# Eleven conversion turns from the last batch to earlier ones, and another order of work in the last batch

## The chip, the cores and the metric

The kernel runs on one core of a Trainium2 chip. The metric is the device time of one execution in microseconds (us), as the median of several runs. Five engines work side by side: TensorE (PE in the profile, PEld for its weight loads), VectorE (DVE), ScalarE (ACT), GpSimd (POOL) and SyncE (SP), which here issues transfers (DMA).

## The reference

Inputs are q, k, v of 8 batches x 8 heads x 576 rows x 64, and weights. Three layers follow one another, in float32:

```python
q_s = softmax(q, over the head's 64);  k_s = softmax(k, over the 576 rows)
x = q_s @ (k_s.T @ v)                      # each head, heads side by side: 576 x 512
h = gelu(x @ w_in)                         # tanh form; w_in is 512 x 1024
u, v = h[..., :512], h[..., 512:]
v_n = (v - mean(v)) / sqrt(var(v) + 1e-6) * g_ln
x = x + (u * (w_sg @ v_n + b_sg)) @ w_out  # w_sg is 576 x 576
xt = x.transpose(0, 2, 1)                  # second block
u = x + (xt @ U @ V).transpose(0, 2, 1)    # U, V of rank 32
out = u + relu(u @ w_ch1) @ w_ch2          # w_ch1 is 512 x 2048
```

The weights arrive as 64-bit floats, so each has to be converted on the chip.

## The kernel before, in words

**Numbers.** Every product is made of three matmuls: an operand is split into a high part (a ScalarE copy to fp32r) and a low part (`low`, a subtraction on VectorE or GpSimd), and high x high, high x low and low x high are added in PSUM (`prod`, line 577).

**Phase one** runs once for each of the 8 batches (`for b in range(B)`, line 1321), each batch in the same stages: the V half of the first product with gelu and statistics (`emit_Vh`, `stats`, `emit_ln`), in 5 tiles of rows; in the same loop, called the passage here, the transposes of the batch before (`emit_yT`), its product with U (`emit_U`, which leaves the tile pst) and with V (`emit_PV`, which leaves PSUM tiles pw, adds them to yt and stores it in `u2d`); then the U half (`emit_Uh`, PSUM tile pu, gelu on ScalarE), the spatial product (`emit_S`, PSUM tile pS; its gate is a multiplication on VectorE, or on GpSimd for the columns in `GATES_POOL`; `split_G` makes the parts gh and gl), and the output product (`emit_y`, PSUM tile py; a VectorE addition makes yt). For the next batch, softmax work, the transposes of q (pt, ql) and the first product (`emit_xT`, px) lie between.

PSUM tiles come from `ps2`, three buffers of two banks (pv, pw, pu, pS, py, pt, px, pm), and `ps1`, two of one bank. A tile's first matmul waits until its buffer's last reader is done.

**Phase two** makes the channel product with seven products instead of eight for each 2 x 2 block: `steps` is a list of 280 steps of 12 matmuls, over five groups of columns, i = 0 for w_ch1 and i = 1 for w_ch2. The letters a = 1 to 7 name the products. A step waits for its weights (`wu`, five buffers, fetched five steps ahead from `wd`). The first seven steps (PSUM tile pm) run in the last batch's part of the loop, mixed with that batch's own transposes and U and V products (`pvs`). Their operands for group 0 (`uh`, `ul`) are made by the generator `u_first` (line 842), called as `prep`, in 26 pieces which the last batch's code takes with `next(prep, None)`. `H_SUMS`, `h_prep` and `u_side` do the same kind of work for later steps.

**Conversions.** w_ch1 and w_ch2 are converted in 16 rounds of 11 items (`conv_ch`): four blocks (load, clamp on GpSimd, exponent on ScalarE, merge in two VectorE instructions, lines 183 and 184) and seven factors (for some a sum on GpSimd or VectorE, then a high part on ScalarE, a low part on GpSimd or VectorE as `DVE_FACTOR_LOWS` says, and a store into `wd`). A turn (`T`) moves the pipeline by one item: it issues one operation of each kind, for items up to six apart (`LATE`). `TURNS[b]` says how many turns stand in each slot of batch b: five slots in the V loop, four each in the U, S and y stages, and up to five in the first product of the next batch; row 0 counts other pieces. `STEP_TURNS` and `GROUP_TURNS` do so for phase two.

**What sets the order.** TensorE runs in written order throughout, VectorE throughout the batches (`in_order(dve)`), all of them in the later steps of phase two. ScalarE, GpSimd and SyncE are otherwise put in order by a planner with its own estimates. Each engine and SyncE's queue run their instructions in order, so one that waits holds those behind it. In this document batches count from 1 to 8; `b` counts from 0.

## Time and profile before

| | before |
|---|---|
| median of 3 runs | 1292.64 us (1290.99 to 1294.96) |
| the profiled execution | 1292.16 us |
| its span, first to last instruction | 1290.4 us |
| TensorE busy | 1261.8 us, 98% |
| VectorE busy | 969.8 us, 75% |
| ScalarE busy | 653.3 us, 51% |
| GpSimd busy | 324.3 us, 25% |
| granted TensorE clock, mean | 0.989 |

The profile is of one execution; times within it count from its first instruction. A busy time says how much of the span an engine worked, not whether anything waited for it; for that the views by stretch and in order of time are needed. By those, batch 8 runs from about 519 us to 586 us, where the first step of phase two starts, and the eighth step starts at 613 us. Ends of matmuls are modelled, so that they overlap their successors, and "idle before" counts from such an end.

### The profile page before, as it was taken

To read this page: it belongs to the slowest core of one execution; us is meant where nothing else is said; L and a number is where in the kernel's file an instruction comes from. 1 tells how busy PE (TensorE), PEld (TensorE's weight loads), DVE (VectorE), ACT (ScalarE), POOL (GpSimd) and SP (SyncE) were. 2 spreads that over 40 slices of the span, in tenths; PEclk is the share of its full clock that TensorE was granted. 3 is DMA by queue.
4 is the path that set the end of the run, shared out by engine and by line. 5 is a ranking of instruction groups with operands and counts; after the bars stand their busy time and mean duration, and the time that the engine had idled before them with its cause. 6 is when DMAs were issued, how large, how long until landed. Compare 5 with 4: busy or idle time off the path is not lost.

```text
span 1290.4 us, 20684 instructions
## 1 busy us (share of the span) xinstructions
PE 1261.8 (98%) x7628; PEld 1142.8 (89%) x7628; DVE 969.8 (75%) x1406; ACT 653.3 (51%) x998; POOL 324.3 (25%) x421
## 2 busy tenths in 40 slices
PE   6999999999999999999999999999999999999998
PEld 5798999999998989797887888888888889999998
DVE  6898889797988888788769943597347953694485
ACT  5756667675757576754563512443224522451342
POOL 4734152623333334663630202000200002000000
PEclk8899999999999999999999999999999999999999
DMA  8515161715343352568998676678766788898786
GB/s 271 167 55 167 51 207 51 235 51 167 99 158 117 113 170 76 195 202 284 397 346 295 213 257 235 220 246 281 259 189 224 256 286 303 274 314 302 256 297 212
DMA packets 135909, 274.17 MB, mean 212 GB/s; under 512 B 15232, under 2 KB 56704, under 8 KB 135808
## 3 DMA queue, kind: packets, MB, share of 16 engines
q1 hardware_dynamic: 135808, 272.84, 64.0%
q8 instruction: 61, 1.00, 0.3%
q14 instruction: 40, 0.33, 0.1%
HBM read 224.56 MB, written 48.23 MB: 211 GB/s over the span
## 4 chain that ended last, share of the span: by engine, by line
PE 82%; DVE 8%; DMA 4%; ACT 3%; issue 1%; POOL 1%; SPq 1%; DVEq 0%; POOLq 0%; ACTq 0%
PE mm L52 51%; PE pS L52 8%; PE py L52 6%; PE pv L52 5%; PE pu L52 5%; PE px L52 1%; PE pk L52 1%; PE pt L553 1%; PE pt L741 1%; PE pp L52 1%; DVE bst L644 1%; DVE sh L654 1%; DMA wu<-wd 1%; DVE yt L55 1%; PE pm L52 1%
## 5 line engine op out<-in xcount | busy, mean ns | idle before, releaser
L52 PE MATMUL mm<-oh,wu 128*128 128x512 f32 (+1 forms) x1120 | 320.5, 367 | 1.2 <-DMA wu<-wd 1.2
L52 PE MATMUL mm<-uh,wu 128*128 128x512 f32 (+1 forms) x1064 | 303.4, 366 | 0.0
L52 PEld LDWEIGHTS mm<-oh,wu 128*128 128x128 f32 x1120 | 207.1, 188 | 27.6 <-ACT oh L61 1.6
L52 PEld LDWEIGHTS mm<-uh,wu 128*128 128x128 f32 x1064 | 196.6, 188 | 24.1 <-issue 0.2
L52 PE MATMUL mm<-ol,wu 128*128 128x512 f32 (+1 forms) x560 | 205.5, 367 | 0.0
L61 ACT ACTIVATE oh<-h 128x1024 fp32r<-128x1024 f32 (+1 forms) x140 | 135.2, 973 | 125.3 <-PE mm L52 104.6
L52 PE MATMUL mm<-ul,wu 128*128 128x512 f32 (+1 forms) x532 | 194.7, 366 | 0.0
L55 DVE TENSOR_TENSOR ol<-h,oh 128x1024 fp32r<-128x1024 f32 (+1 forms) x140 | 156.4, 1121 | 40.1 <-ACT oh L61 37.2
L55 POOL TENSOR_TENSOR ust<-ust 128x1024 f32<-128x1024 f32 (+1 forms) x16 | 36.3, 2278 | 384.5 <-DMA ust<-u2d 323.6
L55 DVE TENSOR_TENSOR h<-mm,u 128x1024 f32<-128x1024 f32 (+1 forms) x57 | 63.3, 1111 | 83.8 <-PE mm L52 83.8
L52 PEld LDWEIGHTS mm<-ol,wu 128*128 128x128 f32 x560 | 105.1, 188 | 13.2
L55 DVE TENSOR_TENSOR u<-mm,u 128x1024 f32<-128x1024 f32 (+1 forms) x53 | 58.9, 1111 | 73.2 <-PE mm L52 68.1
L52 PEld LDWEIGHTS mm<-ul,wu 128*128 128x128 f32 x532 | 99.9, 188 | 12.1
L55 POOL TENSOR_TENSOR chw<-f,chw 128x256 fp32r<-128x256 f32 x98 | 80.7, 836 | 97.6 <-ACT chw L61 87.6
L55 DVE TENSOR_TENSOR h<-h,h 128x1024 f32<-128x1024 f32 (+1 forms) x80 | 88.9, 1111 | 0.1
L1102 ACT ACTIVATE h<-mm 128x1024 f32<-128x1024 f32 (+1 forms) x19 | 17.8, 938 | 128.3 <-PE mm L52 128.3
L1093 ACT ACTIVATE h<-h 128x1024 f32<-128x1024 f32 (+1 forms) x60 | 58.1, 969 | 33.6 <-DVE h L55 33.6
L61 ACT ACTIVATE chw<-f 128x256 fp32r<-128x256 f32 x112 | 42.5, 411 | 63.6 <-DVE f L184 30.7
L61 ACT ACTIVATE u<-mm 128x1024 f32<-128x1024 f32 (+1 forms) x24 | 22.5, 936 | 96.3 <-PE mm L52 80.0
L171 POOL TENSOR_SCALAR stg<-stg 128x256 f32<-128x256 f32 (+1 forms) x88 | 44.3, 508 | 91.3 <-DMA stg<-in_w_ch_dram 50.4
L52 PE MATMUL pu<-xh,wih 128*128 128x288 f32 x256 | 57.9, 308 | 1.9 <-ACT wih L61 0.6
L52 PE MATMUL pu<-xh,wil 128*128 128x288 f32 x256 | 56.3, 301 | 1.8 <-DVE wil L55 1.8
(177 smaller groups left out, 2661.8 us busy)
## 6 DMA issues: line engine op xcount, KB each, us to landing
wu<-wd SPq DMA_DIRECT2D x280, 512.0 KB, 4.4
wd<-chw SPq DMA_DIRECT2D x112, 256.0 KB, 3.5
stg<-in_w_ch_dram SPq DMA_DIRECT2D x64, 256.0 KB, 3.5
u2d<-yt SPq DMA_DIRECT2D x32, 288.0 KB, 2.3
vt<-in_v_dram SPq DMA_DIRECT2D x32, 256.0 KB, 6.9
qt<-in_q_dram SPq DMA_DIRECT2D x7, 1024.0 KB, 8.2
kt<-in_k_dram SPq DMA_DIRECT2D x7, 1024.0 KB, 6.4
res<-u2d SPq DMA_DIRECT2D x12, 512.0 KB, 5.8
```

The source lines that it names most:

```text
L52: pe.matmul(out, lhsT, rhs, start=first, stop=last, skip_group_check=onto)
L55: return eng.tensor_tensor(out=out, in0=a, in1=b, op=op)
L61: return act.activation(out, src, AF.Copy)
L171: eng.tensor_scalar(out=hi, in0=hi, scalar1=F64_MOST, scalar2=-F64_MOST, op0=ALU.min, op1=ALU.max)
L553: pe.transpose(pt[:, t * P : (t + 1) * P], qt[:, t, c * P : (c + 1) * P], ident)
L644: dve.bn_stats(out=bst[0:n], in_=ge[0:n])
L654: dve.scalar_tensor_tensor(out=shift[0:n], in0=mv[0:n, 0:1], scalar=-1.0, in1=mv[0:n, 1:2], op0=ALU.mult, op1=ALU.mult)
L741: pe.transpose(pt[0:n, c * P : (c + 1) * P], y_t[b][:, c, t * P : t * P + n], ident)
L1093: act.activation(h, h, AF.Relu)
L1102: act.activation(h_out(j, 11, n), bank, AF.Relu)
```

## The change

- `TURNS`: batches 2 to 5 get two turns more each and batch 6 three, all in the y stage; the last batch has 18 turns instead of 29, none in its S stage.
- The first slot of the y stage comes behind the first `emit_y` in all batches but the last.
- The last batch gets a branch of its own for the V loop: `emit_U` and `emit_PV` are called right behind `emit_Vh`, ahead of `stats`; the layer norm of tile 2 comes ahead of the slot.
- In the last batch ScalarE is put in written order from the U stage to the y stage (`acts`).
- `GATES_POOL` of the last batch is empty: all four gates on VectorE.
- `emit_y` of the last batch makes columns 0 and 1 together: three of the four parts of both, then the last part of both.
- `u_first` takes tile vh4 instead of vl3 for its fourth operand, and the parts for a = 5 of its second half come behind the low part for a = 4. Its pieces are taken at other places: 1 instead of 3 ahead of the second U product, 5 ahead of the first S product instead of 2 behind it, 1 instead of 2 behind the S stage, and the rest behind step 2's `pvs` instead of within step 2.
- The norm of the last rows (`ln_scale`, `ln_split` of tile 4) comes one U product later.
- Of steps 4 to 6 the turns come behind `pvs`.

```diff
-    GATES_POOL = ((), (2,), (2,), (2,), (2,), (2,), (2,), (2,))
+    GATES_POOL = ((), (2,), (2,), (2,), (2,), (2,), (2,), ())
...
+        cols = (c,) if b < B - 1 or c > 1 else (0, 1)
+        if c == cols[0]:
+            for x in cols:
+                py_t[x] = ps2.tile([P, 2, 512], F32, tag="big", name="py")
+            for fcs in (range(NF - 1), range(NF - 1, NF)):
+                for x in cols:
+                    cs = slice(x * P, (x + 1) * P)
+                    for fc in fcs:
+                        prod(py_t[x], wo_h[:, fc, cs], wo_l[:, fc, cs], gh[:, fc], gl2[:, fc], fc == 0, fc == NF - 1)
+        py = py_t.pop(c)
         tt(dve, two(y_t[b][:, c]), halves(py), two(x_t[b][3][:, c]), ALU.add)
...
-            parts = [wrk.tile([P, F], F32, tag=x, name="us") for x in ("vh2", "vl2", "vh3", "vl3")]
+            parts = [wrk.tile([P, F], F32, tag=x, name="us") for x in ("vh2", "vl2", "vh3", "vh4")]
...
                 tt(dve, u22, u22, u11, ALU.subtract)
-                high(5, u22)
-                yield
-                rest(5, u22)
                 yield
                 rest(4, u21)
+                yield
+                high(5, u22)
+                rest(5, u22)
                 yield
...
-        (('T', '', '', '', ''), ('', '', '', ''), ('T', 'T', 'TTT', 'TT'), ('TT', 'TTTT', 'TTW', ''), ('', '', '', '', '')),
-        (('', '', '', '', ''), ('', '', '', ''), ('', 'TT', 'TT', 'TT'), ('TTT', 'TTTT', 'TT', 'T'), ('', '', '', '', '')),
-        (('', '', '', '', 'T'), ('T', '', '', ''), ('', 'TT', 'TTT', 'TTT'), ('TT', 'TTT', 'T', ''), ('', '', '', '', '')),
-        (('', '', '', '', ''), ('P', '', '', ''), ('', 'TT', 'TT', 'TT'), ('TTT', 'TT', 'TT', 'T'), ('', 'T', '', '', '')),
-        (('', '', '', '', ''), ('', 'B', 'T', 'T'), ('', 'TB', 'TTT', 'TT'), ('T', 'TT', 'TT', 'T'), ('', '', '', '', '')),
+        (('T', '', '', '', ''), ('', '', '', ''), ('T', 'T', 'TTT', 'TT'), ('TT', 'TTTT', 'TTTW', 'T'), ('', '', '', '', '')),
+        (('', '', '', '', ''), ('', '', '', ''), ('', 'TT', 'TT', 'TT'), ('TTT', 'TTTT', 'TTT', 'TT'), ('', '', '', '', '')),
+        (('', '', '', '', 'T'), ('T', '', '', ''), ('', 'TT', 'TTT', 'TTT'), ('TT', 'TTT', 'TT', 'T'), ('', '', '', '', '')),
+        (('', '', '', '', ''), ('P', '', '', ''), ('', 'TT', 'TT', 'TT'), ('TTT', 'TTT', 'TTT', 'T'), ('', 'T', '', '', '')),
+        (('', '', '', '', ''), ('', 'B', 'T', 'T'), ('', 'TB', 'TTT', 'TT'), ('TT', 'TTT', 'TT', 'TT'), ('', '', '', '', '')),
...
-        (('TTT', 'TT', 'TT', 'T', 'TT'), ('TT', 'T', 'T', 'TTT'), ('TT', 'T', 'TT', ''), ('TTT', 'TT', 'PT', 'T')),
+        (('TTT', 'TT', 'TT', '', 'TTT'), ('T', 'T', '', ''), ('', '', '', ''), ('TT', 'TT', 'PT', 'T')),
...
+        else:
+            for t in range(NT + 1):
+                emit_Vh(b, t)
+                if t == 2:
+                    for t2 in range(NT + 1):
+                        emit_U(b - 1, t2)
+                for c in ((), (), (), (0, 1), (2, 3))[t]:
+                    emit_PV(b - 1, c)
                 stats(b, t)
+                if t >= NT - 1:
+                    emit_ln(b, t - 1)
+                slot(TURNS[b][0][t])
+                if 0 < t < NT - 1:
+                    emit_ln(b, t - 1)
                 for t2 in ((2,), (3, 4), (), (), ())[t]:
                     emit_yT(b - 1, t2)
...
+            acts = in_order(act)
+            acts.__enter__()
...
-                for _ in range((0, 3, 3, 3)[f]):
+                for _ in range((0, 1, 3, 3)[f]):
                     next(prep, None)
...
-            if not nxt and f == 1:
+            if not nxt and f == 2:
                 ln_split(b, NT)
...
-            if not nxt and f == 0:
+            if not nxt and f == 1:
                 ln_scale(b, NT)
...
+            if not nxt:
+                for _ in range((5, 0, 0, 0)[f]):
+                    next(prep, None)
             emit_S(b, f)
...
-            if b or c:
+            if c or not nxt:
                 with tc.issue_after(last['s'].ins) if not nxt and c == 0 else contextlib.nullcontext():
                     slot(TURNS[b][3][c])
             emit_y(b, c)
-            if b == 0 and c == 0:
+            if nxt and c == 0:
                 slot(TURNS[b][3][c])
...
+            acts.__exit__(None, None, None)
             close_wo()
...
-                for _ in range((1, 0, 9, 0, 0, 0, 0)[s]):
+                for _ in range((1, 0, 0, 0, 0, 0, 0)[s]):
                     next(prep, None)
-                slot(STEP_TURNS[s])
+                if s < 4:
+                    slot(STEP_TURNS[s])
...
                 pvs(s)
-                for _ in range(2 if s == 1 else 0):
+                for _ in range((0, 2, 9, 0, 0, 0, 0)[s]):
                     next(prep, None)
+                if s >= 4:
+                    slot(STEP_TURNS[s])
```

## Rows read from the trace of the kernel before

**Rows 1.** The page, part 1: busy us (share of the span) and instructions of each engine.

```profile
PE 1261.8 (98%) x7628; PEld 1142.8 (89%) x7628; DVE 969.8 (75%) x1406; ACT 653.3 (51%) x998; POOL 324.3 (25%) x421
```

**Rows 2.** Busy us by stretch (PE, PEld, DVE, ACT, POOL), clock, DMA share, GB/s.

```profile
450.60:519.30 68.70, 68.48 (x531) 64.54 (x530) 59.52 (x113) 46.80 (x79) 26.54 (x37) 1.00 0.41 137
...
519.30:560.00 40.70, 38.50 (x237) 34.26 (x236) 31.25 (x59) 30.78 (x61) 27.38 (x37) 1.00 0.52 178
```

**Rows 3.** TensorE in order of time: start, duration, instruction [idle before, what ended it].

```profile
539.05 0.80 PE L52 MATMUL pw<-v_w,pst 128*128 128x288 f32 x4 [0.26 <-DVE pst L55]
...
543.27 0.53 PE L52 MATMUL pw<-v_w,pst 128*128 128x288 f32 x2 [1.29 <-DVE yt L55]
...
546.70 0.43 PE L52 MATMUL pu<-xl,wih 128*128 128x288 f32 x2
546.96 0.43 PE L52 MATMUL pu<-xh,wil 128*128 128x288 f32 x2
547.85 0.53 PE L52 MATMUL pu<-xh,wih 128*128 128x288 f32 x2 [0.46 <-DVE yt L55]
...
574.99 0.53 PE L52 MATMUL py<-gl,wo_h 128*128 128x288 f32 x2 [0.51 <-DVE gl L55]
...
586.06 0.63 PE L52 MATMUL pm<-uh,wu 128*128 128x512 f32 x2
...
596.94 0.73 PE L52 MATMUL pm<-uh,wu 128*128 128x512 f32 x2 [0.76 <-ACT h L1102]
...
609.24 0.77 PE L52 MATMUL pw<-v_w,pst 128*128 128x288 f32 x2 [0.40 <-DVE yt L55]
```

**Rows 4.** VectorE in order of time, the passage of the last batch.

```profile
537.02 1.25 DVE L654 SCALAR_TENSOR_TENSOR sh<-mv 128x1 f32<-128x1 f32 x1
...
540.96 1.39 DVE L184 SCALAR_TENSOR_TENSOR f<-stg,f 128x256 uint32<-128x256 uint32 x1
...
542.46 1.42 DVE L55 TENSOR_TENSOR yt<-pw,yt 128x576 f32<-128x576 f32 x2
...
547.06 1.40 DVE L55 TENSOR_TENSOR yt<-pw,yt 128x576 f32<-128x576 f32 x2
```

**Rows 5.** GpSimd in order of time, the last batch.

```profile
540.69 1.38 POOL L55 TENSOR_TENSOR vl<-ge,vh 128x512 fp32r<-128x512 f32 x1
...
569.92 1.86 POOL L55 TENSOR_TENSOR gt<-gt,ut 128x576 f32<-128x576 f32 x1 [0.35 <-DVE gt L708]
```

**Rows 6.** VectorE in order of time, the y products of the last batch.

```profile
574.18 1.59 DVE L55 TENSOR_TENSOR gl<-gt,gh 128x576 fp32r<-128x576 f32 x2
...
584.25 0.75 DVE L55 TENSOR_TENSOR yt<-py,x 128x576 f32<-128x576 f32 x1
```

**Rows 7.** ScalarE in order of time, step 2 of phase two.

```profile
595.35 0.63 ACT L61 ACTIVATE uh<-us 128x512 fp32r<-128x512 f32 x1 [1.10 <-DVE us L55]
595.88 1.01 ACT L1102 ACTIVATE h<-pm 128x1024 f32<-128x1024 f32 x1
```

**Rows 8.** The chain that ended last: start, us, what; steps 4 and 5.

```profile
608.15 1.04 DVE yt L55 x2
```

**Rows 9.** Who waited for whom, TensorE: us in total, times, longest.

```profile
PE mm L52 <- DMA wu<-wd: 1.2, 1, 1.2
```

**Rows 10.** Groups of VectorE instructions, batches 2 to 7: count, busy, mean ns, idle before.

```profile
L184 DVE SCALAR_TENSOR_TENSOR f<-stg,f 128x256 uint32<-128x256 uint32 x36 | 18.7, 521 | 1.2
...
L183 DVE TENSOR_SCALAR f<-f 128x256 uint32<-128x256 uint32 x36 | 15.7, 435 | 0.1
...
L55 DVE TENSOR_TENSOR chw<-f,chw 128x256 fp32r<-128x256 f32 x14 | 11.2, 799 | 1.8 <-POOL f L55 1.7
```

**Rows 11.** VectorE in order of time, the y stage of batch 4.

```profile
310.06 0.94 DVE L55 TENSOR_TENSOR chw<-f,chw 128x256 fp32r<-128x256 f32 x1 [1.73 <-POOL f L55]
...
313.80 0.76 DVE L55 TENSOR_TENSOR yt<-py,x 128x576 f32<-128x576 f32 x1 [0.67 <-PE py L52]
```

**Rows 12.** TensorE in order of time, the same stage.

```profile
315.20 0.60 PE L741 MATMUL pt<-ident,yt 128*128 128x128 f32 x4
```

More of the change, by code (lines that the diff above doesn't have):

```diff
@@ L720, in fused_kernel @@
     y_t = {}
+    py_t = {}
     def emit_y(b, c):
@@ L725, in emit_y @@
         gh, gl2 = g_t[b]
-        py = ps2.tile([P, 2, 512], F32, tag="big", name="py")
-        cs = slice(c * P, (c + 1) * P)
-        for fc in range(NF):
-            prod(py, wo_h[:, fc, cs], wo_l[:, fc, cs], gh[:, fc], gl2[:, fc], fc == 0, fc == NF - 1)
+        cols = (c,) if b < B - 1 or c > 1 else (0, 1)
[8 more added lines that the diff above has]
+        py = py_t.pop(c)
         tt(dve, two(y_t[b][:, c]), halves(py), two(x_t[b][3][:, c]), ALU.add)
@@ L1337, in fused_kernel @@
             load_ahead()
-        for t in range(NT + 1):
-            emit_Vh(b, t)
-            if nxt:
-                with behind(dve):
-                    for t2 in Q_MAX[b > 0][t]:
-                        q_max(nxt, t2)
-                    for _ in range(FOLDS[b > 0][t]):
-                        next(fold)
-            if t < NT:
-                stats(b, t)
-            slot(TURNS[b][0][t])
-            if t > 0:
-                emit_ln(b, t - 1)
-            if t == NT:
-                stats(b, t)
-            if b > 0:
+        if nxt:
+            for t in range(NT + 1):
+                emit_Vh(b, t)
+                if nxt:
+                    with behind(dve):
+                        for t2 in Q_MAX[b > 0][t]:
+                            q_max(nxt, t2)
+                        for _ in range(FOLDS[b > 0][t]):
+                            next(fold)
+                if t < NT:
+                    stats(b, t)
+                slot(TURNS[b][0][t])
+                if t > 0:
+                    emit_ln(b, t - 1)
+                if t == NT:
+                    stats(b, t)
+                if b > 0:
+                    for t2 in ((2,), (3, 4), (), (), ())[t]:
+                        emit_yT(b - 1, t2)
+                if t == 2 and b > 0:
+                    for t2 in range(NT + 1):
+                        emit_U(b - 1, t2)
+                if b > 0:
+                    for c in ((), (), (), (0, 1), (2, 3))[t]:
+                        emit_PV(b - 1, c)
+        else:
+            for t in range(NT + 1):
+                emit_Vh(b, t)
+                if t == 2:
+                    for t2 in range(NT + 1):
+                        emit_U(b - 1, t2)
+                for c in ((), (), (), (0, 1), (2, 3))[t]:
+                    emit_PV(b - 1, c)
+                stats(b, t)
+                if t >= NT - 1:
+                    emit_ln(b, t - 1)
+                slot(TURNS[b][0][t])
+                if 0 < t < NT - 1:
+                    emit_ln(b, t - 1)
                 for t2 in ((2,), (3, 4), (), (), ())[t]:
                     emit_yT(b - 1, t2)
-            if t == 2 and b > 0:
-                for t2 in range(NT + 1):
-                    emit_U(b - 1, t2)
-            if b > 0:
-                for c in ((), (), (), (0, 1), (2, 3))[t]:
-                    emit_PV(b - 1, c)
         spread_at = 2 if b else 3
@@ L1447, in fused_kernel @@
                     k_exp(nxt, ((0, 1, 2), (3, 4))[f])
-            if not nxt:
-                for _ in range((2, 0, 0, 0)[f]):
-                    next(prep, None)
             if f > 0:
@@ L1457, in fused_kernel @@
             with tc.issue_after(last['s'].ins):
-                for _ in range(2):
+                for _ in range(1):
                     next(prep, None)
```

## Prediction

> **What bounds the kernel now.** I began with the busy times of the page: TensorE is busy for 98% of the span, the others for 75% or less [rows 1]. A busy TensorE only bounds the whole if it is busy everywhere, so I went on to busy times by stretch. In a middle batch it works 68.48 of 68.70 us: nothing can be won there, and anything that makes it wait is paid in full. In the head of the last batch it works 38.50 of 40.70 us [rows 2]. So the matmul count sets the time, and what a reordering can win is the sum of TensorE's waits from the last batch to the first steps of phase two.
>
> The third view is TensorE's instructions in order of time there, with the idle time ahead of each. Six waits stand out: 0.26 (pw, for VectorE's pst), 1.29 (pw, for VectorE's yt), 0.46 (pu, for yt), 0.51 (py, for gl), 0.76 (pm, for ScalarE's h) and 0.40 us (pw, for yt) [rows 3], 3.68 us in all. Two corrections: ends are modelled, so idle time starts late (pairs at 546.70 and 546.96 start 0.26 us apart though each lasts 0.43, so 0.17 is to be added to each wait), and the first pair after a wait takes 0.53 instead of 0.43 us [rows 3], 0.10 more. With 0.27 for each of six the purse is 3.68 + 1.62 = 5.3 us: 2.82 in the passage (0.26 + 1.29 + 0.46 + 0.81), 0.78 at the y products, 1.03 and 0.67 in the steps. It is 0.41% of the time. Four of the six end with VectorE, so its queue, which is in order, is the second view: what stands in it ahead of the instruction that TensorE waits for.
>
> **Passage reordered, additions first.** The last batch's V loop gets its own branch. TensorE's order stays; what changes is VectorE's. Before, the low part of pst stood behind the shift sh, which took 1.25 us from 537.02 to 538.27; and the first two additions yt stood behind statistics and a conversion merge that took 1.39 us from 540.96; they ran from 542.46 to 543.88. The other two ran at 547.06, behind the statistics of the last tile [rows 4]. Afterwards pst comes ahead of statistics and conversions, the pair of additions right behind V tile 3's products, the next pair right behind tile 4's. The slot of the fourth turn is empty, so no merge stands there. pst then needs no cover: it waits for its own ScalarE copy alone, and I expect its 0.43 us gone. The additions can start when their own pw is there (the first pw runs at 539.05 [rows 3]), if VectorE is free. It has statistics 2, two merges and one sh still to do, which it did before pst in the old order and now does behind it. The pair would so end near 541.5 instead of 543.88, just when pw and pu ask for the PSUM buffers (the pw that waited restarted at 543.27 after 1.29 us idle [rows 3], so it asked near 541.8). The third wait (pu at 547.85) goes too: its addition moves ahead of statistics. What is late next is the statistics and layer-norm of tiles 2 and 3; they are wanted by the S products, which follow four pu groups later, and these cover them. I take 2.3 of 2.82 us, because the two additions come just in time rather than early; bounds 0.8 (one merge and one sh stretched as in [rows 4]: about 0.9 and 1.1 us) and 3.1 (the pu restart after the second pw included).
>
> **Gate 2 of the last batch on VectorE, y products in pairs.** The gate took 1.86 us on GpSimd [rows 5]; a VectorE instruction of that size takes 0.75 us (yt at 584.25 [rows 6]). Because of the late gate two low parts gl came in a bunch, 1.59 us from 574.18 [rows 6], and py waited 0.51 us idle for the first. Now gl of column 2 comes a S group earlier, and py of columns 0 and 1 run three of their four parts (36 matmuls) before they ask for the last gl. Each effect covers the wait alone: 0.75 of 0.78 us, bounds 0.4 and 0.78. The price is that the first y addition is ready later, as its product ends with the pair. Its cover: the second addition, which frees the buffer that pm takes, ended at 585.00 while pm started at 586.06 [rows 3, 6], 1.06 us to spare; one turn and one low part (ul) fewer stand ahead of it now, so I cost it at nothing; without the cover it would cost up to 1 us.
>
> **Preparation of group 0's first operands.** `u_first` keeps its work; five instruction groups come ahead of S product 0 instead of around it, and the a = 5 part of the second half moves behind the fourth low part. In the old order ScalarE copied that uh for 0.53 us (595.35 to 595.88) and only then made h, 1.01 us, for which pm waited 0.76 [rows 3, 7]. Now uh comes behind step 2's transposes. I take 0.55 of 1.03 us: h itself still takes 1.01 us and only the transposes lie beside it; bounds 0 (another ScalarE instruction takes that place) and 1.03. Tile vh4 in place of vl3 and a part one place later cost nothing: step 4, the first to use it, comes a whole step, a round of transposes and the U products later.
>
> **Conversions of steps 4 to 6 behind the additions.** In the chain the pair of yt at 608.15 came just before the pw that waited 0.40 [rows 3, 8], behind a slot of three turns. Additions first: 0.65 of 0.67 us, bounds 0.2 and 0.67. The merges that now come later feed stores alone.
>
> **ScalarE in written order** in the last batch, from the U products to the y products: no instruction more. A wait for a transfer at its head now holds the gelu behind it, and with it a PSUM buffer. ScalarE was busy 30.78 of 40.70 us in that stretch [rows 2], and a U product's gelu has two products' time. I cost it at nothing; bounds: minus 0.5 (the order it replaces delayed h by that) and plus 1.3 us (the longest wait of the stretch).
>
> **Eleven turns to batches 2 to 6.** Eleven turns are one round of the pattern (4 blocks, 7 factors), so batch 7, the head of the last batch and all of phase two meet the same kinds of work at the same slots as before; the last batch has 18 turns instead of 29. Each issues its loads, stores, clamps, copies, merges and lows elsewhere. On VectorE a round costs 4 merges of 0.435 + 0.521 and some three lows of 0.80 us [rows 10], 6.2 us or 0.57 a turn; so 1.1 us in a batch with two more turns, 1.7 with three. They stand in the y stage's slots, the last of them ahead of the fourth y addition. The cover there: VectorE idles 0.67 us ahead of that addition (the smallest of the five batches), and it ends at 314.56 while the transposes that read it start at 315.20 [rows 11, 12]: together 1.31 us. Two turns fit, three only as they spread over several slots. The first slot of the stage moves behind the first y addition; this frees a buffer earlier and costs nothing. I take 0.3 us for all five batches, bounds 0 and 7.6 (below). A gain is excluded: TensorE has no wait there to give back.
>
> **The sum.** 2.3 + 0.75 + 0.55 + 0.65 - 0.3 = 3.95, say 4.0 us. The profiled execution took 1292.16 us (span 1290.4, 1.8 around it), 0.5 below the median 1292.64. 1292.16 - 4.0 = 1288.2.
>
> **The rivals.**
> *Full purse.* All of 5.3 us, and TensorE's one wait in phase two, 1.2 us for a transfer wu [rows 9], goes as well: 1292.2 - 6.5 = 1285.7. For it: two of the cures are doubled. Against: the transfer is behind a burst of loads that the change leaves.
> *Passage half.* VectorE instructions are stretched again ahead of the additions: the merge of 1.39 us ran beside GpSimd's vl, 1.38 us from 540.69 [rows 4, 5]. Then 0.8 instead of 2.3 is won: 1289.7. Such pairs still occur in the new order.
> *The burst takes it back.* If the transfers ahead of the wait for wu [rows 9] are limited by bytes since the last batch, TensorE only comes earlier to the same wait: 0.5 us of gain, 1291.7. Against: fewer conversions lie in the last batch.
> *Slower: stretched turns in batches 2 to 6.* Place: the last slot of the y stage. A merge that meets GpSimd took 1.39 instead of 0.52 us, 0.87 more, and VectorE once waited 1.73 us for a sum on GpSimd [rows 4, 10, 11]. Two turns at 1.1 us, plus 1.7 us for two stretches or for one such wait, make 2.8; beyond the cover of 1.31 stay 1.5 us a batch, 7.6 us in five. 7.6 - 4.25 = 3.4 us lost: 1295.5. It decides from 1.31 us on; where the passage is half as well, it ends at 1297. Against it: VectorE's idle time before that addition is over 0.67 in the other four batches, and most merges meet no GpSimd.
> The Trainium skill, page "Advanced Engine Details and Errata", section "VectorE Performance Modes", says that the second Vector port is shared with GpSimd and that the two block each other; it speaks against more conversion turns beside GpSimd's work. By that rule each added turn meets a block, and the time is that of the slower case; the stretched merge agrees, while the mean of 0.521 us over 36 merges says that most are free [rows 4, 10].
>
> **How the numbers follow.** Forecast (1286.5 to 1289.7) 0.52; full purse 0.14; passage half 0.16; burst 0.06; slower 0.12. The range from 1285.6 to 1291.8 leaves out the slower case and edges. A measurement of this kernel tells about 0.3%, 3.9 us, from no change, so faster means under 1288.8: two thirds of the forecast and the full purse, 0.50; the same: the rest of the forecast, passage half and the burst, 0.38; slower 0.12.
>
> **What would show it.** TensorE's waits for yt, pst and gl between V tile 2 and py gone, h's wait near 0.4 us, pw's in the steps gone; phase two's first step some 3 us earlier, its eighth some 4; the wait for wu about the same length. Batches 2 to 6 still 68.7 us each. I am wrong if these grow, if gelu or px becomes the releaser of a new wait in the last batch, or if the wait for wu grows by what was won.

## The result, and the profile after

The changed kernel takes 1305.8 us (median; 1304.21 to 1307.75), the kernel before 1292.64 (1290.99 to 1294.96): 1.0097 times as long, 95% interval 1.0077 to 1.0118. The forecast was 1288.2, the range ended at 1291.8. The profiled execution has a span of 1305.9 us, 15.5 more than before; it was the longest of the five (1307.75), so the parts below add up to some 2 us more than the medians differ by.

The page, part 1, of the changed kernel, against [rows 1]: TensorE is busy 4.5 us longer with the same 7628 matmuls, VectorE and GpSimd a little less.

```profile
PE 1266.3 (97%) x7628; PEld 1141.2 (87%) x7628; DVE 966.5 (74%) x1408; ACT 654.1 (50%) x998; POOL 318.1 (24%) x419
```

To find the place I cut both traces at the first S product of each batch and measured from one cut to the next. All of the loss lies between the S products of batch 2 and those of batch 7. Busy times by stretch; each stretch runs from the S products of one batch to those of the next, and holds the S and y stages of the first and the V and U stages of the second. The columns are those of [rows 2]. Of the kernel before one of the five and their sum:

```profile
212.46:281.12 68.66, 68.44 (x531) 64.56 (x530) 58.70 (x109) 45.34 (x77) 28.47 (x41) 1.00 0.44 141
...
sum 343.33, PE 342.23 PEld 322.85 DVE 296.10 ACT 223.48 POOL 120.94; mean PE 68.45 PEld 64.57 DVE 59.22 ACT 44.70 POOL 24.19
```

and all five of the changed kernel:

```profile
142.32:216.84 74.52, 70.62 (x532) 65.38 (x530) 61.55 (x111) 46.37 (x80) 31.66 (x46) 0.98 0.42 137
216.84:288.57 71.73, 68.99 (x531) 64.43 (x530) 58.72 (x111) 44.05 (x72) 21.50 (x32) 1.00 0.38 124
288.57:362.31 73.74, 71.17 (x531) 65.61 (x530) 61.81 (x114) 45.10 (x80) 28.75 (x39) 0.98 0.40 134
362.31:433.65 71.34, 69.09 (x531) 64.21 (x530) 59.50 (x113) 46.12 (x74) 21.18 (x31) 1.00 0.40 124
433.65:506.21 72.56, 70.67 (x531) 65.39 (x530) 60.55 (x113) 46.47 (x79) 25.98 (x37) 0.98 0.41 133
sum 363.89, PE 350.55 PEld 325.03 DVE 302.13 ACT 228.11 POOL 129.07; mean PE 70.11 PEld 65.01 DVE 60.43 ACT 45.62 POOL 25.81
```

Read the first two numbers of a row together. Before, TensorE idles 0.2 us in a stretch; now 1.9 to 3.9 us. Where the clock column says 0.98 instead of 1.00 its busy time is longer as well, 70.6 to 71.2 us for the same 531 matmuls instead of 68.4. VectorE has 6.0 us more in the five stretches, about the 6.2 that the prediction gave for a round of eleven turns, and is still busy only 302 of 364 us.

The same cuts for every kernel of this study, each from one profiled execution, in us (e1 to e15 are told below; a step is a step of phase two):

| kernel | five stretches | to S of last batch (passage) | S of last batch to step 0 | seven steps | rest |
|---|---|---|---|---|---|
| before | 343.3 | 70.4 | 28.5 | 27.0 | 677.3 |
| changed | 363.9 | 67.8 | 28.5 | 25.8 | 677.7 |
| e1 order only | 343.7 | 67.2 | 34.9 | 25.8 | 678.5 |
| e2 turns only | 358.1 | 69.0 | 28.5 | 26.9 | 676.0 |
| e3 five buffers | 350.9 | 66.9 | 28.5 | 26.3 | 677.7 |
| e4 turns later | 355.7 | 67.5 | 28.5 | 25.9 | 676.0 |
| e5 before, three buffers | 344.7 | 70.6 | 28.5 | 28.0 | 679.8 |
| e6 passage and steps | 346.5 | 67.5 | 35.7 | 25.8 | 676.6 |
| e7 turns in the S stage | 358.8 | 67.2 | 27.7 | 25.8 | 675.9 |
| e8 steps only | 345.0 | 70.5 | 28.5 | 26.0 | 676.5 |
| e9 turns in phase two | 343.8 | 66.9 | 28.5 | 25.8 | 687.4 |
| e10 one turn each | 350.6 | 69.3 | 29.1 | 27.8 | 677.1 |
| e11 x on VectorE | 370.7 | 69.6 | 28.5 | 26.0 | 677.1 |
| e12 q in another queue | 357.3 | 67.8 | 28.5 | 25.8 | 675.9 |
| e13 before, q in another queue | 344.6 | 70.2 | 28.5 | 27.1 | 677.1 |
| e14 without merges | 356.7 | 67.7 | 28.5 | 27.8 | 676.5 |
| e15 without merges, q moved | 352.6 | 67.7 | 28.5 | 27.8 | 677.4 |

What is left to the span is the time to the S products of batch 2: 143.8 us before, 142.3 after. The change does not touch the code of that stretch, and it lies between 143.3 and 148.9 us in the other kernels (152.7 in e3), so 1.5 us there mean nothing. The kernels whose batches 2 to 6 have the old turns take 343.3 to 346.5 us in the five stretches, so differences up to 3 us there are not read either.

**What happens in a stretch.** ScalarE of the changed kernel in order of time, from the end of the y stage of batch 6 into the V stage of batch 7:

```profile
469.27 0.44 ACT L61 ACTIVATE chw<-f 128x256 fp32r<-128x256 f32 x1
...
469.91 0.61 ACT L61 ACTIVATE yh<-pt 128x512 fp32r<-128x512 f32 x1
472.66 0.42 ACT L61 ACTIVATE chw<-f 128x256 fp32r<-128x256 f32 x1 [2.14 <-DMA wd<-chw]
472.98 1.17 ACT L61 ACTIVATE xh<-px 128x576 fp32r<-128x576 f32 x2
```

Then TensorE and VectorE at the same time, and the DMA queue of SyncE ahead of it:

```profile
473.67 0.51 PE L52 MATMUL pv<-wih,xh 128*128 128x512 f32 x1 [1.61 <-ACT xh L61]
473.65 0.76 DVE L55 TENSOR_TENSOR xl<-px,xh 128x576 fp32r<-128x576 f32 x1 [2.40 <-ACT xh L61]
463.23 0.39 SPq L133 DMA_DIRECT2D qt<-in_q_dram  x1
463.71 0.64 SPq L134 DMA_DIRECT2D qt<-in_q_dram  x1
465.39 3.31 SPq L384 DMA_DIRECT2D wd<-chw  x3
```

There are four chw buffers (they hold a factor's high and low part until they are stored), and a factor's copy needs one whose store has landed. A conversion copy stands in ScalarE's queue ahead of the copies xh of the next batch's operand; it waits 2.14 us for the store issued at 465.39, right behind the load of q (1 MB and 128 KB), xh waits behind it, and TensorE and VectorE both wait for xh. In the trace each of the five waits of such copies for a store stands ahead of a copy xh. The waits from 107 to 520 us, which cover the five stretches (us in total, times, longest):

```profile
ACT chw L61 <- DMA wd<-chw: 11.4, 5, 3.2
PE pv L52 <- ACT xh L61: 7.3, 5, 2.0
PE pv L52 <- DVE xl L55: 2.1, 4, 0.7
PE pu L52 <- DVE yt L55: 1.1, 1, 1.1
```

Before, in the same window, ScalarE waited once for a store, and no pv waited for xh:

```profile
ACT chw L61 <- DMA wd<-chw: 1.4, 1, 1.4
```

**The clock.** The granted clock behind that wait, by 2 us, and then a batch where the wait for xh was 0.86 us:

```profile
473.00:475.00 2.00, 1.28 (x4) 0.78 (x5) 1.03 (x2) 2.00 (x5) 1.12 (x2) 1.00 1.05 356
475.00:477.00 2.00, 2.00 (x8) 1.27 (x7) 2.00 (x4) 1.98 (x4) 0.40 (x1) 0.50 1.01 356
477.00:479.00 2.00, 2.00 (x7) 1.62 (x7) 1.80 (x5) 1.44 (x3) 0.00 (x0) 0.65 1.17 304
...
258.00:260.00 2.00, 1.78 (x10) 1.52 (x11) 2.00 (x5) 1.98 (x3) 0.41 (x1) 1.00 0.93 307
```

0.50 is the level of 1.2 GHz instead of 2.4. It came after waits of 2.04, 1.88 and 1.61 us, in the three stretches with 0.98 in the table, and not after those of 0.86 and 0.87. Half of 2 us and 0.35 of the next 2 are 1.7 us of TensorE's time, nearly as much again as the wait ahead of it. The length of a wait alone does not settle whether the clock falls, as other runs below show: in e14 it fell behind one of two waits of 1.27 us, and in e7 it stayed at 1.00 behind one of 2.30 us (in e10 of 2.20, in e13 of 1.90):

```profile
311.69 0.53 PE L52 MATMUL py<-gh,wo_h 128*128 128x288 f32 x2 [2.30 <-DVE ql L55]
...
313.60:315.60 2.00, 2.00 (x18) 2.00 (x17) 1.97 (x4) 1.08 (x2) 1.33 (x2) 1.00 0.00 1
```

So of the 20.5 us in the five stretches 12.2 are idle time of TensorE (13.3 against 1.1 us), 5.1 the three falls of the clock, and 3.2 longer busy time besides.

**The last batch and the steps** went about as forecast. Who waited for whom, TensorE, from the V loop of the last batch to the end of the steps, all of it (before: five kinds, 3.8 us):

```profile
PE pm L52 <- ACT h L1109: 0.6, 1, 0.6
PE py L52 <- DVE gl L55: 0.5, 1, 0.5
PE py L52 <- DVE ql L55: 0.3, 1, 0.3
```

The waits for yt and pst of [rows 3] are gone: VectorE's two pairs of additions [rows 4] now run back to back with their products,

```profile
559.58 1.42 DVE L55 TENSOR_TENSOR yt<-pw,yt 128x576 f32<-128x576 f32 x2
562.59 1.41 DVE L55 TENSOR_TENSOR yt<-pw,yt 128x576 f32<-128x576 f32 x2
```

while py still waits as long as before [rows 3, 6]: the last gate and the pair of gl on VectorE, and TensorE behind them,

```profile
589.93 0.76 DVE L55 TENSOR_TENSOR gt<-gt,ut 128x576 f32<-128x576 f32 x1
590.61 1.59 DVE L55 TENSOR_TENSOR gl<-gt,gh 128x576 fp32r<-128x576 f32 x2
591.41 0.53 PE L52 MATMUL py<-gl,wo_h 128*128 128x288 f32 x2 [0.51 <-DVE gl L55]
```

h still makes pm wait 0.64 us (0.76 in [rows 3]), and the transfer wu 0.49 and, far later, 0.70 us (one wait of 1.2 in [rows 9]).

### The profile page after: what moved, and what is told of

Read it like the earlier page. It is cut to its first block, busy times and chain, and to the rows that moved or that the text cites. A ratio compares the mean times of both kernels' runs of the same rounds, so it can differ in the third digit from the quotient of the medians.

```text
span 1305.9 us, 20686 instructions
## 1 busy us (share of the span) xinstructions
PE 1266.3 (97%) x7628; PEld 1141.2 (87%) x7628; DVE 966.5 (74%) x1408; ACT 654.1 (50%) x998; POOL 318.1 (24%) x419
## 4 chain that ended last, share of the span: by engine, by line
PE 74%; DVE 10%; DMA 6%; ACT 5%; POOL 2%; issue 2%; SPq 1%; DVEq 0%; ACTq 0%; POOLq 0%
PE mm L52 50%; PE pS L52 6%; PE pv L52 6%; PE pu L52 4%; PE py L52 3%; DMA wd<-chw 3%; DMA wu<-wd 1%; PE pm L52 1%; PE pp L52 1%; DVE f L183 1%; PE pt L748 1%; DVE bst L644 1%; DVE sh L654 1%; DVE f L184 1%; POOL chw L55 1%
## 5 line engine op out<-in xcount | busy, mean ns | idle before, releaser
L55 POOL TENSOR_TENSOR chw<-f,chw 128x256 fp32r<-128x256 f32 x95 | 76.1, 812 | 107.6 <-ACT chw L61 106.0
L52 PE MATMUL pv<-wih,xh 128*128 128x512 f32 x128 | 54.6, 427 | 7.3 <-ACT xh L61 7.3
L52 PE MATMUL py<-gh,wo_h 128*128 128x288 f32 x256 | 56.8, 303 | 2.3 <-DVE gt L708 1.6
```

The source lines that it names most:

```text
L52: pe.matmul(out, lhsT, rhs, start=first, stop=last, skip_group_check=onto)
L55: return eng.tensor_tensor(out=out, in0=a, in1=b, op=op)
```

## The experiments

In the kernel before, `prod` stands at line 563, `u_first` at 836 and the loop over the batches at 1324.

### Which part of the change costs the time

**e1**: the changed kernel with the old rows of turns; **e2**: the kernel before with the new ones (the same edit the other way round).

```diff
-    TURNS = ( ... 'TTTW', 'T' ... 'TTT', 'TT' ... )   # e1
+    TURNS = ( ... 'TTW', ''  ... 'TT', 'T'  ... )
```

> The changed kernel with the turns of the kernel before (all 29 in the last batch). Buffer theory: the 20.6 us that batches 2 to 6 lost in the changed kernel come from the eleven added turns, whose ScalarE copy into chw waits for a store and holds the copies xh behind it. Then batches 2 to 6 take 68.7 us again and no pv waits for xh; of the gain of the last batch and the steps (2.65 + 1.2 us in the trace after) a part stays: 1288 to 1291 us. Slot theory (the first slot of the y stage, moved behind the first y product, does the harm): still 1300 us or more, with batches of 70 to 74 us.

> The kernel before with the turns of the changed one and nothing else. Buffer theory: batches 2 to 6 lose about 20 us as in the changed kernel, the last batch wins 0 to 2 us by 11 turns fewer: 1308 to 1313 us. Slot theory: 1290 to 1293 us, batches of 68.7 us.

e1 takes 1295.17 us, ratio 1.0011 (0.9998 to 1.0025); e2 1303.5, ratio 1.0068 (1.0044 to 1.0092). So the turns carry the loss. The five stretches say where: 343.7 us in e1, 358.1 in e2. e2 is better there than the changed kernel by 5.8 us. The only other difference in these batches is the first slot of the y stage behind the first y product, which alone costs 0.3 us (e1); that it costs more where turns are added is likely, but not shown, as each number is of one execution.

e1 also shows what the eleven turns were in the way of. It wins the passage (67.2) and the steps (25.8), but loses 6.4 us at the y products. In order of time in e1: on VectorE the second of two merges ahead of a gate of the S stage, and TensorE's two waits for the low parts gl:

```profile
568.76 0.43 DVE L184 SCALAR_TENSOR_TENSOR f<-stg,f 128x256 uint32<-128x256 uint32 x1
569.10 0.81 DVE L708 SCALAR_TENSOR_TENSOR gt<-pS,gl,bb 128x576 f32<-128x576 f32 x1
...
574.38 0.53 PE L52 MATMUL py<-gl,wo_h 128*128 128x288 f32 x2 [1.89 <-DVE gl L55]
577.44 0.85 PE L52 MATMUL py<-gl,wo_h 128*128 128x288 f32 x2 [1.91 <-DVE gl L55]
```

and the granted clock behind them (the first number after the busy times):

```profile
577.00:579.00 2.00, 1.56 (x6) 1.56 (x7) 1.92 (x4) 2.00 (x5) 0.00 (x0) 0.50 0.92 268
```

**e6**: the kernel before with the new V loop, the new steps and `u_first`, without the moved turns, the written order of ScalarE, the pair of products and the gate. **e8**: the new steps and `u_first` alone.

```diff
...
+        else:
+            for t in range(NT + 1):
+                emit_Vh(b, t)
...
-                slot(STEP_TURNS[s])
+                if s < 4:
+                    slot(STEP_TURNS[s])
```

> The kernel before with the changed V loop of the last batch, the changed order of the seven steps and of u_first's last parts (vh4 with them), without the moved turns, ScalarE's written order, the gate, the pair of columns and the five pieces ahead of S. Theory: what the changed kernel won in the last batch lies in these parts alone, 2.65 us in the passage and 1.2 us in the steps, and it needs no turn moved: 1288 to 1290 us, S to the first step 28.5 us as before. Rival: the passage wins only because 11 turns fewer stand in the last batch: 1291 to 1294 us.

> The kernel before with the new order of the steps alone (additions ahead of the conversions in steps 4 to 6, the a = 5 part of the second half of the first operands one place later, tile vh4). Theory (backlog): the loss of 6 to 7 us at the last batch's y products in the two runs with the new passage and 29 turns comes from the reordered V loop, which this run leaves as it was; so the stretch from the S products to the first step stays at 28.5 us, the seven steps fall from 26.97 to 25.8, batches 2 to 7 stay at 68.7 and 70.4, and the time is 1292.6 - 1.2 = 1291.4. Rival: that loss comes from the changed first operands and steps; then the stretch grows to 35 us and the time is near 1297.7.

e6: 1296.25 us, ratio 1.0023 (1.0011 to 1.0035); passage and steps win the same, the y products lose 7.2 us. Their longest wait is another one than in e1: py waits 2.7 us for ScalarE's copies gh, which stand behind a copy uh that waits 4.40 us for the load of us. e8: 1292.45, ratio 0.9997 (0.9985 to 1.001); the steps are 1.0 us shorter and the y products stay at 28.5. e8 differs from e6 by the passage alone. So the gain of the steps is free, that of the passage is paid again at the y products unless turns leave the last batch. e8 is the best kernel here; what it wins is too small to be told from no change.

### ScalarE's queue

**e5**: the kernel before with three chw buffers instead of four: the wait for stores alone. **e3**: the changed kernel with five, and for the space one staging buffer for loaded weights less (four instead of five).

```diff
-    chw = [((stgp, 4),), 0]
+    chw = [((stgp, 5),), 0]   # e3
...
```

> The kernel before with three chw buffers instead of four and nothing else: no turn is moved. Buffer theory: ScalarE's copies into chw now wait for stores in the y stages of this kernel too (1.4 us in all with four), hold the xh copies, and the batches take 70 to 74 us as with the added turns: 1298 to 1310 us. Number theory (two turns a batch are too much work for VectorE, GpSimd or the transfers): the work is the same as before, so 1290 to 1295 us.

> The changed kernel with five buffers for the factors' high and low parts (chw) instead of four; for the space, four instead of five for loaded stages. Buffer theory: the copy that waited for the store of four factors before now waits for none or for one stored earlier; most of 20.6 us comes back: 1285 to 1292 us, ScalarE's waits of chw for wd stores under 3 us instead of 11.4 in batches 2 to 6. VectorE theory (the added merges and lows fill VectorE in the y stage): unchanged, 1304 to 1308 us. A start slower by 1 to 2 us for the fourth stage buffer is possible under both.

e5: 1301.03 us, ratio 1.0058 (1.0042 to 1.0073). That time lies in the buffer theory's range, but the execution that was profiled was the shortest (1296.68), and its five stretches took 344.7 us, not 70 to 74 each; where the longer ones spent 4 to 5 us more is not known. Its waits for stores (107 to 520 us) are as long in sum as those of the changed kernel, though spread over more copies:

```profile
ACT chw L61 <- DMA wd<-chw: 11.1, 13, 3.2
```

and no pv waits for xh: the longest, 3.2 us, stands ahead of work that TensorE did not wait for, and the one just ahead of an xh is 0.7 us. A long wait for a store cost nothing by itself in that execution. e3: 1306.05 us, ratio 1.0099 (1.0072 to 1.0127); the kernel loses 9 us before the S products of batch 2, so the time says little, but the five stretches fall to 350.9 us. Its waits:

```profile
ACT chw L61 <- DMA wd<-chw: 3.5, 2, 2.7
PE pv L52 <- ACT x L61: 1.3, 1, 1.3
```

pv's waits for xh are gone, and no clock falls in these stretches. The wait that is left is of the same kind with another releaser: the copy x stands behind a conversion's exponent, which waits 2.39 us for GpSimd. 7.6 us of 20.5 stay.

**e4**: all eleven added turns in the last slot of the same batches, behind the next batch's first product, instead of in the y stage. **e7**: in the S stage (and the pair of y products of columns 0 and 1 split after two parts of four instead of three).

```diff
...
-  ('TT', 'TTTT', 'TTTW', 'T'), ('', '', '', '', '')
+  ('TT', 'TTTT', 'TTW', ''), ('', '', '', '', 'TT')   # e4
...
```

> The changed kernel with the eleven added turns in the last slot of the same batches, behind the next batch's first product (px, its copies xh and x) instead of in the y stage. Buffer theory: the same copies may still wait for stores, but behind xh and not ahead of it, so pv no longer waits for xh: 1286 to 1293 us. Number theory (two turns more a batch are too many wherever they stand, for VectorE or the transfers): 1300 us or more.

> The changed kernel with the eleven added turns in the S stages of the same batches, whose ScalarE has idle time and which lie ahead of the loads of q, k and v; and with the pair of py columns split after two parts of four instead of three. Buffer theory: no xh waits in batches 2 to 6, which take 68.7 to 70 us: 1287 to 1293 us. Number theory: still 70 to 74 us a batch, 1300 us or more. The split: py's wait for gl (0.51 us idle in the changed kernel) goes, S to the first step 27.7 instead of 28.5 us, since that gl stands behind the last gate on VectorE and has nothing to do with GpSimd.

e4: 1300.04 us, ratio 1.0052 (1.0032 to 1.0072); pw waits 3.5 us for yt in the next V stage, pv 1.1 for xh; five stretches 355.7. e7: 1302.57, ratio 1.0069 (1.0052 to 1.0086); py waits 3.3 us for ql; 358.8. The loss moves with the turns, and most of it stays: 12.4 and 15.5 of 20.5 us. On the side e7 shows that py's wait for gl is a matter of the split: 27.7 instead of 28.5 us.

**e10**: one added turn in each of the five batches, none in the last slot; six are back in the last batch. **e11**: all turns as in the changed kernel, but the copies out of px 2 and 3 on VectorE, so that xh has no chw copy ahead of it.

```diff
-        high = copy(two(xh[:, c]), halves(px))
+        late = b > 0 and c >= 2
+        high = (dve.tensor_copy if late else copy)(two(xh[:, c]), halves(px))
...
```

> The changed kernel with one added turn in each of batches 2 to 6 in place of two or three, none in the y stage's last slot beyond what the kernel before has there; the other six are back in the last batch (five in its S stage, one behind a U product). Theory (order of ScalarE's queue): a copy into a chw buffer stands ahead of the copies xh only through the last slots; without that the five batches together take 343.3 + 0 to 3 us, and pv has no wait for xh. Rival (number): the loss goes with the number of turns, 5/11 of 20.5 us, so 352 to 353 us. Both: the last batch's y products lose some part of the 6 to 7 us that 29 turns cost them, so 1290 to 1297 by the one, 1299 to 1306 by the other.

> The changed kernel, all turns where it has them; the four copies out of the products px 2 and 3 of the next batch (xh and x) run on VectorE, which idled 2 us there, instead of ScalarE: what TensorE waits for no longer stands behind a copy that waits for a store. The waits of ScalarE for stores stay. Theory (order of ScalarE's queue): pv's waits for xh go and with them the low clock behind them; the five batches fall from 363.9 to 345 to 352 us (VectorE has 2.8 us more in each), the time to 1287 to 1294. Rival (number of turns, VectorE as the limit): 2.8 us more on VectorE in each batch make it worse, 364 us or more and 1306 or more.

e10: 1300.68 us, ratio 1.0062 (1.0045 to 1.0078). No pv waits for xh, as the first theory has it, but the five stretches take 350.6 us, nearer to the rival's 352. Four of them lose 0.4 to 1.1 us, together no more than what is not read here, and one loses 4.6, where px waited 2.20 us for xl. That wait too began in ScalarE's queue: xl waited for the copy x, which stood behind a conversion copy that waited for a sum on GpSimd. ScalarE, then VectorE:

```profile
390.21 0.42 ACT L61 ACTIVATE chw<-f 128x256 fp32r<-128x256 f32 x1 [1.75 <-POOL f L55]
390.53 0.63 ACT L61 ACTIVATE x<-px 128x576 f32<-128x576 f32 x1
...
391.19 0.76 DVE L55 TENSOR_TENSOR xl<-px,xh 128x576 fp32r<-128x576 f32 x1 [3.44 <-ACT x L61]
```

So even one turn in a batch can cost, and a store is not the only thing that a copy ahead of x or xh can wait for.

e11: 1317.87 us, ratio 1.0178 (1.0152 to 1.0204), the worst of all; the five stretches take 370.7. The theory that ScalarE's order alone makes the loss forecast 345 to 352 us and fails here, though not cleanly, as the edit also loads VectorE. Waits from 107 to 520 us (the first of the six for xl lies ahead of the five stretches):

```profile
ACT chw L61 <- DMA wd<-chw: 20.6, 9, 4.8
PE pv L52 <- DVE xl L55: 7.6, 6, 1.3
PE pv L52 <- DVE xh L592: 3.4, 8, 2.2
```

VectorE was busy 83% of the time in the changed kernel and idle just where xh was late, and still cannot take these copies (2.3 us more a stretch): TensorE waits for it, and ScalarE waits longer for stores, 20.6 us, whose low parts and sums partly run on VectorE.

### Stores and VectorE taken away one by one

**e12**: the changed kernel with the loads of q through ScalarE's DMA queue, so that no store stands behind them. **e13**: the same edit on the kernel before.

```diff
-            sp.dma_start(qt[:, t : t + step, :], src)
+            (act if b > 1 else sp).dma_start(qt[:, t : t + step, :], src)
...
```

> The changed kernel with the loads of q for batches 3 to 8 (1 MB and 128 KB each) issued through ScalarE's DMA queue instead of SyncE's; all turns where the changed kernel has them, no engine has more to compute. In the changed kernel the store that ScalarE waits for stands right behind such a load in SyncE's queue and lands 7.2 us after its issue (4.1 in the median). Theory (the store lands late because of the load ahead of it in one queue): ScalarE's waits of 2 to 3.2 us for stores shrink to 1 us or less, pv's waits for xh go, the five batches take 345 to 352 us, and the time is 1287 to 1295. Rival (bytes: both share the same 16 DMA engines whatever the queue): landing times stay at 7 us, the five batches at 360 us or more, the time at 1302 to 1308. Second rival (number of turns): the waits for stores shrink but others (xl, yt, ql) take their place, 353 to 360 us, 1295 to 1302.

> The kernel before with the same loads of q through ScalarE's queue: what that edit does by itself. All theories: the five batches stay within 1 us of 343.3 and the time within 3 us of 1292.6; more than that would have to be taken off the run with the changed kernel.

e13: 1293.74 us, ratio 1.0001 (0.999 to 1.0011), so the edit by itself changes nothing that can be measured. e12: 1301.03, ratio 1.006 (1.0045 to 1.0075), 4.8 us better than the changed kernel; the five stretches 357.3, 6.6 less, the second rival's range. Waits:

```profile
ACT chw L61 <- DMA wd<-chw: 8.9, 7, 2.0
PE pv L52 <- ACT xh L61: 4.5, 4, 1.6
```

The longest wait for a store falls from 3.2 to 2.0 us, and no stretch has a clock under 1.00 any more. Of the 6.6 us 5.1 are the three falls of the clock that do not come, and 2.0 are idle time (11.4 instead of 13.3). As a wait's length does not settle whether the clock falls (here it stayed at 1.00 behind 1.62 us for xh), the 5.1 may in part be chance. The Trainium skill, page "DMA: Bandwidth & Descriptors", section "Queues, rings and completion order", says that a DMA engine takes turns between the queues that have work and takes up a queue's descriptors in order. The landing times show little of it: the median store in these batches took about as long as before, 3.6 against 3.4 us, and the first store behind each of the five loads of q took 7.5, 5.6, 7.0, 8.3 and 6.8 us against 9.9, 5.7, 5.9, 8.2 and 7.2 in the changed kernel. In that the rival of the bytes had it right: a store beside a load of q lands late in either queue.

**e14**: the changed kernel without the merge of the first block in each y stage of batches 2 to 7, which brings VectorE back to the work it had before (296.5 us in the five stretches). **e15**: e14 with the loads of q as in e12.

```diff
-            self.keep[self.a] = from_f64(self.w, self.t)
+            if Block.skip:
+                Block.skip = False
+                self.keep[self.a] = self.t
+            else:
+                self.keep[self.a] = from_f64(self.w, self.t)
...
```

> The changed kernel with the merge of the first block in each y stage of batches 2 to 7 left out (two VectorE instructions of 0.96 us together; the output is without them); loads, copies, lows and stores stay. VectorE then has about the work of the kernel before in these batches (302 us in five, minus 4.8). Theory (VectorE's queue is what the turns fill): waits for yt and xl and the copies that wait for a merged f go, the five batches take 345 to 352 us. Rival (stores): ScalarE's waits for stores stay as long as 2 to 3 us, pv waits for xh behind them, and the five batches stay at 357 to 365 us.

> The same with the loads of q through ScalarE's queue, which alone took the five batches from 363.9 to 357.3. Theory (VectorE and stores together make the loss): 343.5 to 347 us for the five batches. Rival (copies and lows on ScalarE and GpSimd, or the order of the plan, have a part of their own): 350 us or more.

e14: 1303.86 us, ratio 1.0079 (1.0062 to 1.0095); five stretches 356.7, under the rival's 357 by a hair and far from the 345 to 352 of the theory. e15: 1301.93, ratio 1.0063 (1.0042 to 1.0083); 352.6, on the rival's side too (350 or more). Waits of e14 from 107 to 520 us:

```profile
ACT chw L61 <- DMA wd<-chw: 6.9, 5, 2.1
PE pv L52 <- ACT xh L61: 2.5, 2, 1.3
PE pw L52 <- DVE yt L55: 1.9, 2, 1.4
```

With less on VectorE the waits for stores shrink too, from 11.4 to 6.9 us. That fits one chain, in which a merged f, its copy, its low part and its store follow each other through three engines and a queue, but no run takes the links apart. By the stretches the left-out merges and the moved loads of q take 11.3 of 20.5 us away together, 6.2 of idle time and 5.1 of the clock; 9.3 stay, for what else a turn brings and for the order that the plan gives it. The times alone can't tell e12, e14 and e15 apart, their intervals overlap; the steps of e14 and e15 are also 2 us longer than those of the changed kernel.

### Elsewhere

**e9**: the changed kernel with batches 2 to 6 as before and the eleven turns in the first steps of phase two.

```diff
-    GROUP_TURNS = (2, 2, 2, 2, 2, 2, 2, 2, 2, 2, 3, 3, 2, 3, ...)
+    GROUP_TURNS = (3, 3, 3, 3, 3, 3, 3, 3, 3, 3, 3, 3, 3, 3, ...)
```

> The changed kernel with batches 2 to 6 as in the kernel before, and the eleven turns in the first steps of phase two (one more in eleven of them) instead of in these batches. Theory (order of ScalarE's queue): the loss of 20.5 us lies in the five batches alone, which go back to 68.7 us each; the passage stays at 67.7 us and the seven steps at 25.8; with the y products of the last batch at 28.5 the time is 1292.6 - 2.7 - 1.2 = 1288.7, if phase two has room. Rival (transfers): the first 75 us of phase two move 350 to 400 GB/s in the kernel before, eleven turns are 11 transfers of 256 KB, 2.8 MB or 7 us at that rate; TensorE's wait for wu (1.2 us there) grows by up to 7 us: 1288.7 to 1295.7.

1299.73 us, ratio 1.0052 (1.0037 to 1.0066). The five stretches are back at 343.8, passage and steps keep their gain, and phase two gives 10.1 us back. TensorE's waits from 612 to 700 us:

```profile
PE mm L52 <- DMA wu<-wd: 5.2, 3, 2.4
PE mm L52 <- DVE h L55: 2.6, 2, 1.5
```

The rival with the transfers had their part: the wait for wu grew by 4.0 us, from 1.2 to 5.2, within its 7. Its time, 1295.7 at most, is passed all the same: that VectorE's h is late as well it did not have, nor a fall of the clock behind these waits (0.94 in the mean from 640 to 670 us).

## Why the prediction was wrong, point by point

- **Passage**: forecast 2.3 us, measured 2.66. Right; all three waits are gone.
- **Gate on VectorE and pairs of y products**: forecast 0.75, measured 0.05. The step named the late gate on GpSimd as the cause of the bunch of two gl. The bunch is still there at 590.61 without GpSimd, as in VectorE's written order gl of column 2 stands behind the gate of column 3. e7 won the wait by another split.
- **First operands, and the additions of the steps**: forecast 0.55 + 0.65 = 1.2, the seven steps measured 1.19. Right in sum, and e8 has 1.0 of it alone; but pm's wait for h, which was to give 0.55, went from 0.76 to 0.64 only, so that the sum came out is partly luck. The wait for yt went whole.
- **ScalarE in written order**: forecast nothing; no wait behind it is seen in the last batch. e6 without it wins the same passage and steps, but waits 2.7 us for gh behind a load, a wait which e1 with it does not have; so it may be worth something when 29 turns stand there. No run tests it alone.
- **Eleven turns to batches 2 to 6**: forecast 0.3 with bounds 0 and 7.6, measured 20.5 in the profiled execution (some 17 by the medians: 13.2 lost and 3.9 won elsewhere). This step failed, and it decides the sign; batches 2 to 6 at 68.7 us were the prediction's own sign, and they take 71.3 to 74.5. It priced a turn by VectorE alone, 0.57 us, and looked for cover ahead of one VectorE addition [rows 11, 12]; the VectorE work was right (6.0 measured, 6.2 forecast), the cover was not what counted. A turn also puts a copy into ScalarE's queue that needs a buffer whose store has landed, and a store behind a 1.1 MB load. The prediction itself names the loads, stores, clamps, copies, merges and lows of a turn, and priced only the merges and lows on VectorE. Its upper bound had no term for the clock either, 1.7 us for each fall, 5.1 in all. e1 and e2 show that the turns are the cause; the trace of the changed kernel shows the wait for xh behind such a copy in each of the five stretches, e3 that a fifth buffer takes it away, and e12 to e15 that 11.3 us go with the left-out merges and the moved loads of q.
- **The slower rival** had the place and the sign, with 12 in 100, and the wrong mechanism: VectorE's merges stretched by GpSimd. They were not stretched. The group of merges on VectorE in the five stretches (count, busy, mean ns, idle before):

```profile
L184 DVE SCALAR_TENSOR_TENSOR f<-stg,f 128x256 uint32<-128x256 uint32 x32 | 16.2, 505 | 1.1
```

The mean is 505 ns, against 533 for the 28 merges of the kernel before in the same stretches and 521 in [rows 10]. The Trainium skill, page "Advanced Engine Details and Errata", section "VectorE Performance Modes", says that instructions of GpSimd and Vector instructions in a two-port mode block each other. Read as a block for each added turn, as the rival read it, that is not what these rows show.

- **Not foreseen at all**: that the reordered passage makes the eleven turns impossible to leave in the last batch (e1, e6: 6.4 and 7.2 us at the y products), so the two halves of the change hang together. The prediction said that the pu groups would cover the statistics, layer norms and merges pushed behind the additions. With 29 turns that cover looks too small in e1, where merges stand ahead of the gates; in e6 the longest wait is the one for gh, so how much of the loss this explains stays open.

What stays open: how the remaining 9.3 us divide among the copies on ScalarE, the low parts and sums on GpSimd, and the order of the plan, and what decides whether the clock falls behind a wait. No kernel here beats the one before by a margin that can be measured.

## What to carry to other kernels

Before work is moved into a stage whose bounding engine is busy 68.48 of 68.70 us, follow one unit of that work through every engine and queue, and ask at each which instruction of the critical path stands behind it, and what buffer it needs free. Busy shares of the other engines that leave time over (86% on VectorE and 65% on ScalarE here, before the change) say little about room, when the stage has an order of its own with a due time every few microseconds. And add to the price of a wait of TensorE what the clock may take behind it, here up to 1.7 us, as a chance and not as a certainty.

## What the hardware did that I had not expected

In the changed kernel the granted clock fell to 0.50 behind single waits for operands of 1.61 to 2.04 us in the middle of dense matmuls, and was at 0.65 to 0.74 in the next 2 us; behind waits of 0.86 and 0.87 us it stayed at 1.00. It is no matter of length alone: it fell behind 1.27 us in e14 and stayed at 1.00 behind 2.30 us in e7. And a 256 KB store issued right behind a load of 1.1 MB took 7.2 us from issue to landing, where the median of all stores of the kernel is 4.1; with that load in another queue its counterpart in e12 still took 6.8.
